# Idle products as planned and only wide, and the combinations of w_out on VectorE

## The chip, the cores and the metric

The kernel runs on one core of a Trainium2 chip. The metric is the device time of one execution in microseconds, taken as the median of several runs. A separate execution was recorded by the hardware profiler; its page and its trace are what is read here. TensorE appears in them as PE (its weight loads as PEld), VectorE as DVE, ScalarE as ACT, GpSimd as POOL, and SyncE, which here only issues DMAs, as SP. "Issue" is time in which an engine waited for nothing that the profile shows.

## The reference

A recurrent attention block feeds a dense block. For each of 4 batches and 8 heads, 768 steps go through a 48 x 48 state; the 3072 rows of the result (384 wide) then go through two weight matrices with a pointwise function between them. The weights come as 64-bit floats.

```python
for t in range(S):
    kt, vt, rt = (k[:, :, t], v[:, :, t], r[:, :, t])
    cur = np.einsum('bhd,bhe->bhde', u[None] * kt, vt)
    y[:, :, t] = np.einsum('bhd,bhde->bhe', rt, state + cur)
    state = w[None, :, :, None] * state + np.einsum('bhd,bhe->bhde', kt, vt)
...
h = x @ w_in                  # 3072 x 384 by 384 x 2048
g = h - np.tanh(h)
return (g @ w_out).astype(np.float32)   # 2048 x 384
```

## The kernel before

**Units.** The recurrence is cut into 64 steps of two batches: a unit, 24 in all. The function `unit` gives each its steps. TensorE turns r and k (L738); VectorE scales r by powers of the decay (L742), ScalarE copies k (L751) or VectorE scales it (L746). TensorE makes the products with the state and the levels, k against r within the 64 steps (both L693). VectorE copies the levels under a mask into `at` (L892), ScalarE writes the diagonal of `at` (L763). TensorE then makes the outputs and the state's increment (L693), ScalarE copies the output into `xt` and `rest` (L829), GpSimd issues six DMAs for every two units that move `rest` into place (L850), and VectorE adds to the state and decays it (L856, L901). Two states alternate, and all units share the product banks `yk_ps` and, for the first sixteen, `x_ps`. So the units run one behind the other.

**Dense tiles.** Two units make one column block j of 256 tokens, 12 in all. A tile is one j with two groups of 128 rows of the hidden layer. TensorE makes `h` in two halves (L166, three products each), ScalarE five functions of it (L175 to L183), VectorE four operations that end in `g` (L190 to L196; L190 reads `h` in PSUM, L192 and L194 read two SBUF tiles), and TensorE the product with `w_out` into `o` (L204). `h` has two banks, so the tile after next needs this tile's `h` read. The first six j are done in four passes over quarters of the hidden layer, with sums kept in `part` (L217). The last six j use seven products instead of eight (L254, banks `p`): GpSimd adds pieces of `g` into `sg` (L239 to L243), and combinations of `w_out`, called `mixed`, are made once for all, in 16 operations (`mixing`, L263; `mix` holds the formulas). `mixed` takes the place of the buffers of the weights' conversion, so it is made after the last conversion.

**Weights.** Sixteen pieces are loaded as 64-bit numbers by SP and GpSimd (L121) and made 32-bit floats by five operations of VectorE and two of ScalarE each (L135 to L141).

**The order.** Every step is put on a list with its engine, its cost and what it waits for (`add`). The class `Plan` then finds an order by hand-written simulation when the program is built: `forward` lays the steps out by due times, `order` tries 1000 random changes of these times and keeps those that end no later. Each engine's instructions stand in that order; nothing is reordered while the kernel runs. SP's loads are steps of the plan too, and each load waits for the one eight places ahead of it on its engine to land.

**Idle products.** In the opening TensorE has gaps, and the plan puts products into them whose result nobody reads (`fills`), into an `h` bank until the first `h`, then into an `x_ps` bank until the first `o`. There are wide ones of 512 columns (L630, `w_up` against the identity, planned at 0.9 us), which need `w_up`, and narrow ones of 128 (L631, identity against itself, planned at 0.25). `filled` counts how many fit between the end of the last step on TensorE and the start of the next. `forward` also plans TensorE's instruction fetch: it counts steps, and where a block of them ends, the end of the step can be put later:

```python
late = max(0.0, comes - crossed)
end += late
...
free[e] = end
```

When the plan is written out at the end of `order`, the gap is counted a second time, from

```python
free = t.start + t.cost
```

which is without `late`.

Of the kernel before, what the change touches and what calls it, by code (L numbers as in the profile page):

```python
# [143 lines left out]
class Dense:  # L144
# [112 lines left out]
    def mix(self, f, x):  # L257

        n, w, pairs = self.d.DM // 2, self.w_out_sb.rearrange("p (f z) n -> p f z n", z=2)[:, f], self.seven.mixed[:, f]
        b11, b12, b21, b22 = w[:, :, 0, :n], w[:, :, 0, n:], w[:, :, 1, :n], w[:, :, 1, n:]  # L260
        out, a, b, op = [(0, b11, b12, ALU.subtract), (1, b22, pairs[:, :, 0], ALU.add), (2, b22, b12, ALU.subtract),
                         (3, pairs[:, :, 1], b21, ALU.subtract)][x]
        self.nc.gpsimd.tensor_tensor(pairs[:, :, out], a, b, op)  # L263

    def collect(self, t, x):

# [29 lines left out]
class Plan:  # L296
# [14 lines left out]
    def add(self, engine, cost, run, after=(), due=1e9, data=0, gated=False, steps=0):  # L311
        t = SimpleNamespace(engine=engine, cost=cost, run=run, after=[x for x in after if x], due=due, data=data,
                            gated=gated, steps=steps, then=[], n=len(self.tasks))
        for x in t.after:
            x.then.append(t)
        self.tasks.append(t)
        return t
# [12 lines left out]
    def forward(self, due):  # L330

        ready = [max(self.FIRST, due[t.n] - self.EARLY) if t.gated else 0.0 for t in self.tasks]
        count = [len(t.after) for t in self.tasks]
        waiting = self.queues(ready, count)
        free, lanes, channel = dict(self.BEGIN), {}, 0.0
        step, bound, comes, fills = 0, self.CHUNK_0, 0.0, iter(self.fills)
        filling = next(fills, None)
        starts, done, last, first, changed = [None] * len(ready), [], 0.0, {}, set(waiting)
        while len(done) < len(ready):
            for e in changed:  # L340
                ts = waiting[e]
                first.pop(e, None)
                if not ts:
                    continue
                start = max(free.get(e, 0.0), min(ready[x.n] for x in ts))
                t = min((x for x in ts if ready[x.n] <= start + 1e-9), key=lambda x: (due[x.n], x.n))
                if t.data:
                    start = max(start, lanes.setdefault(e, [0.0] * self.LANES)[0])
                else:

                    soon = [x for x in ts if ready[x.n] < start + t.cost and due[x.n] < due[t.n] - self.SPARE]
                    if soon:
                        t = min(soon, key=lambda x: (ready[x.n], x.n))
                        start = max(start, ready[t.n])
                first[e] = start, t
            e = min(first, key=lambda x: (first[x][0], x))
            start, t = first[e]
            waiting[e].remove(t)
            changed = {e}
            end = start + t.cost  # L360
            if e == "PE":
                if filling:
                    step += 4 * len(self.filled(filling, free[e], start, starts))
                    if t is filling[1]:
                        filling = next(fills, None)
                step += t.steps
                if step >= bound:
                    each = t.cost / max(t.steps, 1)
                    crossed = end - (step - bound) * each
                    late = max(0.0, comes - crossed)  # L370
                    end += late
                    comes = max(crossed + late + self.ASKED * each + .3, channel) + self.COMES
                    bound += self.CHUNK
            free[e] = end
            if t.data:
                channel = max(channel, start + 1.2) + t.data
                end = max(end + self.LANDS, channel + self.LANDED) + self.slow(start)
                lanes[e] = lanes[e][1:] + [end]
            starts[t.n] = start
            last = max(last, end)  # L380
            done.append(t)
            for x in t.then:
                ready[x.n] = max(ready[x.n], end + self.hop(t, x))
                count[x.n] -= 1
                if not count[x.n]:
                    waiting[x.engine].append(x)
                    changed.add(x.engine)
        return last, starts, done
# [47 lines left out]
    def order(self, tries=1000):  # L436


        due = [t.due for t in self.tasks]
        for t in reversed(self.tasks):  # L440
            for x in t.then:
                due[t.n] = min(due[t.n], due[x.n] - t.cost - self.HOP - (self.LANDS if t.data else 0))
        plan = self.forward(due)
        for _ in range(4):
            due = self.backward(plan)
            plan = self.forward(due)
        chance = Random(5)
        for _ in range(tries):
            by, at, wide = chance.choice((0.3, 1, 2, 5)), chance.uniform(0, plan[0]), chance.choice((15, 40, 100, 700))
            moved = [x + chance.gauss(0, by) * (abs(start - at) < wide / 2) for x, start in zip(due, plan[1])]  # L450
            other = self.forward(moved)
            if chance.random() < .5:
                latest = self.backward(other)
                again = self.forward(latest)
                if again[0] < other[0]:
                    other, moved = again, latest
            if other[0] <= plan[0]:
                plan, due = other, moved
        self.due = due
        _, starts, done = plan  # L460
        free, order, fills = self.BEGIN["PE"], [], iter(self.fills)
        filling = next(fills, None)
        for t in done:
            t.start = starts[t.n]
            if t.engine == "PE" and filling:
                order += [SimpleNamespace(engine="PE", cost=0.0, start=free, run=run)
                          for run in self.filled(filling, free, t.start, starts)]
                if t is filling[1]:
                    filling = next(fills, None)
                free = t.start + t.cost  # L470
            order.append(t)
        return order

# [18 lines left out]
def near(ctx, tc, r, k, v, w, u, out, shared, moe_w_in, moe_w_out):  # L492
# [3 lines left out]
    V, A, T, G, Q = nc.vector, nc.scalar, nc.tensor, nc.gpsimd, nc.sync  # L496
    d = shared["dims"]
    H, D, NP, NK, B, HEAD = d.H, d.D, d.NP, d.NK, d.B, d.HEAD
    ident = shared["ident"]
# [13 lines left out]
    plan = Plan()  # L513
    add = plan.add
# [87 lines left out]
    w_up = fixed("w_up", [128, NP, 2, SHORT])  # L602
# [7 lines left out]
    idle, tab = (ps_d.tile([128, 2, d.NT], F32, name="h", tag="h") for _ in range(2))  # L610
    idle, tab = idle.rearrange("d z t -> d (z t)"), tab.rearrange("s z t -> s (z t)")
# [14 lines left out]


    def fills(to):
        wide = w_up.rearrange("d p z t -> d (p z t)")
        return [(.9, lambda: T.matmul(to, ident, wide, start=True, stop=True)),  # L630
                (.25, lambda: T.matmul(to[:, :128], ident, ident, start=True, stop=True))]  # L631


    now = [add(e, 1.25 if e == "ACT" else .87, lambda e=e, at=at, x=x: e_of[e].dma_start(out=rows[at : at + NP, :, :D], in_=x.rearrange("(p i) d -> p i d", i=2)), due=-1, data=.05)
           for e, at, x in (("SP", 0, w), ("ACT", NP, u))]
# [3 lines left out]
    now = add("DVE", .45, lambda: V.tensor_scalar(  # L639
        by[:, :, 1:], wcol[:, :, None].to_broadcast([128, NP, SHORT]), W_LOW, W_HIGH, ALU.max, ALU.min), [cols])  # L640
# [3 lines left out]
    ups = add("ACT", .6, lambda: A.copy(w_up, power[:, :, None, :SHORT].to_broadcast([128, NP, 2, SHORT])), [now])  # L644
# [28 lines left out]
    loads, converted = [], []  # L673
# [238 lines left out]
    def mixing():  # L912

        for f in range(0, d.NF // 2, 2):
            now = None
            for x in range(4):
                def run(f=f, x=x):
                    later()
                    dense.mix(slice(f, f + 2), x)

                now = add("POOL", 1.0, run, converted + [now])
            mixed.append(now)

    def finished_seven(t, x, due, pace):
# [11 lines left out]
    def hidden(j, fs, f, due, pace, seven=False):  # L936
# [8 lines left out]
        x.h = add("PE", 1.29, lambda: dense.h(t, 1), [now], due + 1.3, steps=12)  # L945
        last_h[j] = x.h
        if m == 0:
            plan.fills += [([], tabled, fills(idle)[1:]), ([ups], now, fills(idle))]
        x.s = add("ACT", .48, lambda: dense.act(t, "s"), [x.h, b2.c1, b2.q, b2.small, b1.s])
        x.th = add("ACT", .48, lambda: dense.act(t, "th"), [x.h, b2.g, b1.th] + ([units[m].rk, units[m].kw] if m < L else []))  # L950
        x.tg = add("ACT", .48, lambda: dense.act(t, "tg"), [x.h, b2.cp, b1.tg])
# [23 lines left out]
        for i in range(L):  # L975
            ends = SimpleNamespace()

            def run(i=i, ends=ends):
                dense.empty(t, i)
                ends.o = t.o  # L980
# [346 lines left out]
```

## Time and profile before

| | |
|---|---|
| median of 3 runs | 617.49 us (616.53 to 619.28) |
| profiled execution | 616.69 us |
| its span, first to last instruction | 615.0 us |
| mean granted TensorE clock | 0.991 |
| idle products, L631 / L630 | 72 passes of 128 / 24 passes of 512 |
| `mixed` on GpSimd, L263 | 16 operations in three groups: 10.9, 5.7 and 5.4 us busy |
| VectorE operation of the same shape, L867 | 0.58 us mean |

How to read it: a 32-bit product runs in two passes on TensorE, and the trace counts passes, so 72 passes are 36 products. A line of a timeline gives the start, the time until the last of its instructions ended, engine, line, operation, output and inputs, and in brackets the idle time before it with what ended it. A line of a table by stretches gives the stretch and its length, then busy time and number of instructions of PE, PEld, DVE, ACT and POOL, the granted clock, the DMA share and GB/s. A line of the waits gives the total, how often, and the longest.

### The profile page before, as it was taken

To read this page: it belongs to the slowest core of one execution; us is meant where nothing else is said; L and a number is where in the kernel's file an instruction comes from. 1 tells how busy PE (TensorE), PEld (TensorE's weight loads), DVE (VectorE), ACT (ScalarE), POOL (GpSimd) and SP (SyncE) were. 2 spreads that over 40 slices of the span, in tenths; PEclk is the share of its full clock that TensorE was granted. 3 is DMA by queue.
4 is the path that set the end of the run, shared out by engine and by line. 5 is a ranking of instruction groups with operands and counts; after the bars stand their busy time and mean duration, and the time that the engine had idled before them with its cause. 6 is when DMAs were issued, how large, how long until landed. Compare 5 with 4: busy or idle time off the path is not lost.

```text
span 615.0 us, 13927 instructions
## 1 busy us (share of the span) xinstructions
PE 596.4 (97%) x5499; PEld 483.4 (79%) x5499; DVE 453.5 (74%) x735; ACT 401.9 (65%) x896; POOL 177.1 (29%) x313
## 2 busy tenths in 40 slices
PE   8799999999999999997999999999999999999995
PEld 7477777667777777775777799889889899889993
DVE  5599888997789689996668765766786765645753
ACT  2498878878676567662557765675775666747652
POOL 5001311300000000193123452543362244436440
PEclk9899999999999999997999999999999999999999
DMA  7964686407024100002123410130120010100101
GB/s 128 219 126 88 129 161 166 90 0 174 8 46 102 52 0 2 0 14 52 38 52 82 82 23 0 37 57 19 26 58 17 15 27 7 23 6 8 26 2 30
DMA packets 86323, 33.73 MB, mean 55 GB/s; under 512 B 78537, under 2 KB 80681, under 8 KB 86249
## 3 DMA queue, kind: packets, MB, share of 16 engines
q1 hardware_dynamic: 81084, 25.57, 20.7%
q0 software_dynamic: 4992, 6.99, 5.2%
q8 instruction: 45, 0.74, 0.5%
q14 instruction: 30, 0.24, 0.1%
q10 hardware_dynamic: 172, 0.20, 0.1%
HBM read 26.94 MB, written 4.72 MB: 51 GB/s over the span
## 4 chain that ended last, share of the span: by engine, by line
PE 79%; DVE 9%; ACT 5%; issue 3%; DMA 2%; SPq 1%; DVEq 0%; ACTq 0%
PE h L166 36%; PE p L254 17%; PE o L204 16%; PE yk_ps L693 5%; DVE rT L742 1%; DVE tg L194 1%; PE yk_ps L738 1%; DVE tg L192 1%; PE h L630 1%; SPq L726 1%; ACT at L763 1%; PE p L204 1%; PE x_ps L738 1%; DVE g L196 1%; DMA kt<-in_k_dram 1%
## 5 line engine op out<-in xcount | busy, mean ns | idle before, releaser
L166 PE MATMUL h<-xt,w_in_sb 128*128 128x256 f32 x1152 | 282.4, 382 | 0.2 <-DVE w_in_sb L141 0.2
L166 PEld LDWEIGHTS h<-xt,w_in_sb 128*128 128x128 f32 x1152 | 214.6, 191 | 42.7 <-issue 1.0
L204 PE MATMUL o<-w_out_sb,g 128*128 128x384 f32 x384 | 142.0, 493 | 0.5 <-DVE g L196 0.3
L192 DVE SCALAR_TENSOR_TENSOR tg<-s,tg 128x512 f32<-128x512 f32 x96 | 68.7, 716 | 58.8 <-ACT tg L179 44.4
L190 DVE TENSOR_TENSOR g<-h,th 128x512 f32<-128x512 f32 x96 | 65.9, 686 | 43.0 <-ACT s L175 32.2
L204 PEld LDWEIGHTS o<-w_out_sb,g 128*128 128x128 f32 x384 | 72.0, 191 | 32.5 <-DVE g L196 1.4
L179 ACT ACTIVATE tg<-h 128x512 f32<-128x512 f32 x96 | 57.2, 595 | 53.7 <-PE h L166 53.7
L175 ACT ACTIVATE s<-h 128x512 f32<-128x512 f32 x96 | 57.3, 596 | 49.7 <-PE h L166 49.7
L177 ACT ACTIVATE th<-h 128x512 f32<-128x512 f32 x96 | 57.1, 595 | 32.0 <-PE h L166 31.9
L196 DVE COPY_PREDICATED g<-small,tg 128x512 f32<-128x512 int32 x96 | 73.2, 763 | 5.0
L194 DVE SCALAR_TENSOR_TENSOR tg<-q,tg 128x512 f32<-128x512 f32 x96 | 69.6, 725 | 6.1 <-ACT q L181 2.6
L239 POOL TENSOR_TENSOR sg<-g 128x256 f32<-128x256 f32 x46 | 35.2, 766 | 132.3 <-DVE g L196 123.0
L181 ACT ACTIVATE q<-s,m1b 128x512 f32<-128x512 f32 x96 | 69.5, 724 | 0.5
L183 ACT ACTIVATE small<-s,smallb 128x512 f32<-128x512 f32 x96 | 69.4, 723 | 0.5
L254 PE MATMUL p<-mixed,sg 128*128 128x192 f32 x276 | 67.4, 326 | 0.0
L850 POOL DMA_DIRECT2D xt<-rest x66 | 32.4, 497 | 91.8 <-ACT rest L829 91.6
L763 ACT ACTIVATE at<-same,du 128x64 f32<-128x64 f32 x184 | 47.6, 341 | 4.9 <-DVE du L759 4.7
L254 PEld LDWEIGHTS p<-mixed,sg 128*128 128x128 f32 x276 | 48.7, 190 | 0.0
L254 PE MATMUL p<-w_out_sb,g 128*128 128x192 f32 x184 | 46.2, 333 | 0.0
L254 PEld LDWEIGHTS p<-w_out_sb,g 128*128 128x128 f32 x184 | 33.2, 190 | 4.3
L263 POOL TENSOR_TENSOR mixed<-w_out_sb 128x384 f32<-128x384 f32 x8 | 10.9, 1378 | 77.2 <-DVE w_out_sb L141 77.2
L829 ACT COPY xt<-yk_ps 64x192 f32<-64x192 f32 (+2 forms) x50 | 16.2, 323 | 23.7 <-PE yk_ps L693 23.3
(136 smaller groups left out, 694.4 us busy)
## 6 DMA issues: line engine op xcount, KB each, us to landing
st<-in_moe_w_out_dram SPq DMA_DIRECT2D x8, 768.0 KB, 7.3
rt<-in_r_dram SPq DMA_DIRECT2D x48, 96.0 KB, 2.9
vt<-in_v_dram SPq DMA_DIRECT2D x48, 96.0 KB, 3.0
st<-in_moe_w_in_dram SPq DMA_DIRECT2D x16, 288.0 KB, 6.4
kt<-in_k_dram SPq DMA_DIRECT2D x44, 96.0 KB, 2.9
out_dram<-part POOLq DMA_DIRECT2D x24, 96.0 KB, 2.2
out_dram<-o POOLq DMA_DIRECT2D x20, 96.0 KB, 2.1
st<-in_moe_w_in_dram POOLq DMA_DIRECT2D x16, 96.0 KB, 3.9
```

What stands on the lines that cost most here:

```text
L166: self.nc.tensor.matmul(t.h2[:, z], self.w_in_sb[:, t.f // 2, kk, z * 128 : (z + 1) * 128], self.xts[t.j][:, kk].rearrange("p b t -> p (b ...
L175: A.activation(out, t.h, AF.Square)
L177: A.activation(out, t.h, AF.Tanh)
L179: A.activation(out, t.h, AF.Tanh, scale=G1)
L181: A.activation(out, t.s, AF.Square, bias=self.m1b)
L183: A.activation(out, t.s, AF.Relu, bias=self.smallb, scale=-1.0)
L190: V.tensor_tensor(t.g, t.h, t.th, ALU.subtract)
L192: V.scalar_tensor_tensor(t.tg, t.s, C4, t.tg, ALU.mult, ALU.mult)
L194: V.scalar_tensor_tensor(t.tg, t.q, K1, t.tg, ALU.add, ALU.mult)
L196: V.copy_predicated(t.g, t.small.bitcast(I32), t.tg)
L204: self.nc.tensor.matmul(self.outs[i], t.g2[:, z, i * C : (i + 1) * C], self.w_out_sb[:, t.f + z, :], start=t.first and z == 0, stop=t.last ...
L254: self.nc.tensor.matmul(ps[bank][:, half * n : (half + 1) * n], a, b, start=t.first and half == 0, stop=t.last, skip_group_check=True)
```

## The change

Three things are done. `order` runs `forward` once more on the times it chose, and `forward` keeps for each step of TensorE which idle products it counted in front of it (`fitted`); these are the ones written out. The idle products become 512 columns (planned at 0.9) or 256 columns (planned at 0.46), both the identity against itself repeated, so they need no `w_up` and come from one list from the start to the first `h`. And the 16 combinations of `w_out` are steps of VectorE, planned at 0.47 each, instead of GpSimd, planned at 1.0. Since costs and steps differ, the search ends in another order of all engines' instructions.

```diff
@@ mix
-        self.nc.gpsimd.tensor_tensor(pairs[:, :, out], a, b, op)
+        self.nc.vector.tensor_tensor(pairs[:, :, out], a, b, op)
@@ forward
+        self.fitted = []
...
                 if filling:
-                    step += 4 * len(self.filled(filling, free[e], start, starts))
+                    runs = self.filled(filling, free[e], start, starts)
+                    self.fitted.append((free[e], t.n, runs))
+                    step += 4 * len(runs)
@@ order
-        free, order, fills = self.BEGIN["PE"], [], iter(self.fills)
-        filling = next(fills, None)
+        self.forward(due)
+        fitted, order = {n: (free, runs) for free, n, runs in self.fitted}, []
         for t in done:
             t.start = starts[t.n]
-            if t.engine == "PE" and filling:
-                order += [SimpleNamespace(engine="PE", cost=0.0, start=free, run=run)
-                          for run in self.filled(filling, free, t.start, starts)]
-                if t is filling[1]:
-                    filling = next(fills, None)
-                free = t.start + t.cost
+            free, runs = fitted.get(t.n, (0.0, [])) if t.engine == "PE" else (0.0, [])
+            order += [SimpleNamespace(engine="PE", cost=0.0, start=free, run=run) for run in runs]
             order.append(t)
@@ fills
-        wide = w_up.rearrange("d p z t -> d (p z t)")
-        return [(.9, lambda: T.matmul(to, ident, wide, start=True, stop=True)),
-                (.25, lambda: T.matmul(to[:, :128], ident, ident, start=True, stop=True))]
+        def run(n):
+            T.matmul(to[:, : n * 128].rearrange("p (n m) -> p n m", n=n), ident, ident[:, None, :].to_broadcast([128, n, 128]),
+                     start=True, stop=True)
+
+        return [(.9, lambda: run(4)), (.46, lambda: run(2))]
@@ mixing
-                now = add("POOL", 1.0, run, converted + [now])
+                now = add("DVE", .47, run, converted + [now])
@@ hidden
-            plan.fills += [([], tabled, fills(idle)[1:]), ([ups], now, fills(idle))]
+            plan.fills.append(([], now, fills(idle)))
```

## The prediction

> **What bounds the kernel now.** I read the page's busy shares first, then the waits of the matmul queue, then busy time by stretch, and at last the timelines where a stretch is not full.
>
> ```profile
> PE 596.4 (97%) x5499; PEld 483.4 (79%) x5499; DVE 453.5 (74%) x735; ACT 401.9 (65%) x896; POOL 177.1 (29%) x313
> ```
>
> TensorE is busy nearly always, and its real work is not changed. So only three things can move: idle products, TensorE's idle time, and work at a lowered clock. Its waits, longest in total first:
>
> ```profile
> PE yk_ps L693 <- DVE at L892: 4.0, 3, 3.3
> PE x_ps L693 <- issue: 3.7, 1, 3.7
> ```
>
> Two single waits stand out. The first, by stretches of 4 us (columns: PE, PEld, DVE, ACT, POOL busy, then granted clock):
>
> ```profile
> 276.00:280.00 4.00, 4.00 (x75) 2.75 (x74) 4.00 (x5) 0.96 (x2) 4.00 (x4) 1.00 0.00 0
> 280.00:284.00 4.00, 0.65 (x6) 0.07 (x6) 3.96 (x7) 0.00 (x0) 1.36 (x3) 0.92 0.00 0
> 284.00:288.00 4.00, 4.00 (x68) 3.00 (x69) 1.33 (x3) 2.00 (x8) 1.22 (x3) 0.50 0.59 127
> 288.00:292.00 4.00, 4.00 (x13) 2.79 (x12) 0.59 (x2) 1.67 (x7) 0.00 (x0) 0.73 0.41 74
> ```
>
> TensorE idles while VectorE is full, and then runs at half clock. The timelines (VectorE, then TensorE) say why:
>
> ```profile
> 267.74 0.69 DVE L190 TENSOR_TENSOR g<-h,th 128x512 f32<-128x512 f32 x1 [0.33 <-ACT tg L179]
> 268.35 1.46 DVE L192 SCALAR_TENSOR_TENSOR tg<-s,tg 128x512 f32<-128x512 f32 x1
> 269.92 1.30 DVE L194 SCALAR_TENSOR_TENSOR tg<-q,tg 128x512 f32<-128x512 f32 x1
> ...
> 291.97 0.69 DVE L192 SCALAR_TENSOR_TENSOR tg<-s,tg 128x512 f32<-128x512 f32 x1 [2.84 <-ACT tg L179]
> ```
> ```profile
> 283.93 1.14 PE L693 MATMUL yk_ps<-at,vt 64*64 64x64 f32 x32 [3.35 <-DVE at L892]
> 284.85 1.05 PE L693 MATMUL yk_ps<-vt,kw 64*64 64x48 f32 x32
> 285.83 2.93 PE L204 MATMUL o<-w_out_sb,g 128*128 128x384 f32 x4
> 288.55 2.27 PE L166 MATMUL h<-xt,w_in_sb 128*128 128x256 f32 x6
> ```
>
> While GpSimd makes `mixed` (258.96 to 280.4), VectorE's products of two SBUF tiles take up to 1.46 us instead of 0.69; L190, with one operand in PSUM, stays at 0.69. VectorE falls behind and the copy L892 comes late.
>
> The second wait, in TensorE's timeline:
>
> ```profile
> 16.17 0.34 PE L693 MATMUL x_ps<-rT,kT 48*64 48x64 f32 x6
> 20.20 0.77 PE L693 MATMUL x_ps<-rT,kT 48*64 48x64 f32 x26 [3.70 <-issue]
> 20.91 6.90 PE L630 MATMUL h<-w_up,ident 128*128 128x512 f32 x12
> 27.65 0.38 PE L631 MATMUL h<-ident 128*128 128x128 f32 x2
> 27.96 0.58 PE L693 MATMUL yk_ps<-at,vt 64*64 64x64 f32 x24
> ```
>
> TensorE stops within unit 1's levels with nothing that the profile shows to wait for, then runs six wide idle products, although unit 1's copy L892 was done at 22.2 (21.48 + 0.72). They hold the unit for 5.8 us.
>
> **What the Trainium skill says.** "GPSIMD Engine Reference", § 8 Key points: GpSimd shares SBUF interfaces with VectorE, contending with instructions in a two-port mode or with two SBUF inputs. The trace agrees (1.46 against 0.69, L190 untouched). "TensorE: Matmul & The Clock Gate", What's actually happening: an idle window of about 3.4 us halves the clock, about 3.4 us of work restores it. Here 3.35 us idle gave 0.50, and 1.00 came back by 292. "Runtime: NRT & Kernel Launch", Instruction fetch mechanics: instructions come in blocks of 256, mostly hidden. Here one fetch, as I read the wait, cost 3.70 us.
>
> **The combinations move to VectorE.** Removed: 16 GpSimd operations, 10.9 + 5.7 + 5.4 = 22.0 us busy (three groups of L263), on no path of their own. What they cost is the 3.35 us wait plus the slow work after it: 64 passes of L693 in 1.96 instead of 1.15, an `o` pair in 2.86 instead of 1.29, an `h` half in 2.06 instead of 1.29 (chain of waits), together 0.81 + 1.57 + 0.77 = 3.15. In sum 6.5 us. Added: 16 VectorE operations of 128x384, two SBUF inputs. The nearest row is L867, 0.55 to 0.58 us each and 0.47 from start to start when queued: 16 x 0.47 to 16 x 0.58 = 7.5 to 9.3 us. By the order of the built program they stand one to four at a time between five dense tiles. A tile costs TensorE 4 x 1.29 = 5.17 us there, and VectorE 4 x 0.62 + 2 x 0.47 + 4 x 0.47 = 5.3: even. Between the end of a tile's `h` and its `o`, the new order has 12.9 us of TensorE work (before, in its mixing stretch: 5.2 to 7.8), so a lag of a tenth of a microsecond a tile is covered. Without that cover it would cost up to 9.3; I take 0. GpSimd's queue loses operations that stood ahead of output DMAs only. Gain: 6.5 (bounds 3.3, if the clock still falls for another reason, and 6.5).
>
> **The idle products.** Before: 36 of 128 columns and 12 of 512, 10,752 columns. After: 13 of 512 and 8 of 256, 8,704. The first 1,024 columns, at half clock, are equal and take 3.7 us in both (1.52 to 5.24). The other 2,048 go at 1.79 us for eight of 128 (7.75 to 9.54), 3.6 us; and the six behind the fetch ran slow, 6.74 instead of 6 x 0.9. Some 4.9 us of filling go, and idle time may take its place; so I walk the units by hand, with the durations above.
> Up to the stop TensorE had made 219 passes, 46 of them idle products; now those are 16. The stop therefore comes 30 passes later, behind unit 1's levels, in the idle products that follow. If the block lands at about 20.2 as before, unit 1's outputs start near 20.5 instead of 27.96. Then unit 2's state products near 25.5 (32.26 before); its outputs near 28.1 (37.71), held by VectorE's second L135, which waits for weights that SP now issues near 18.5, behind the operands of units 1 and 2; I let them land at 25.3. Next the first `h`, both halves, near 30.7, behind L141; unit 3 at 33.3 (43.37); unit 4 at 40.5 (50.95); the last idle product ends near 42.4 (53.09 before).
> Not all of that is gain. At unit 4 the new order has two `h` halves less done (2.6 us), and from there VectorE sets the pace: in 40 to 53 it was busy 12.73 of 13, in 53 to 70 16.53 of 17. In my walk the first `o` comes at 51.5, with about 4.8 us more of TensorE work done than before at that time, and before then lost 1.1 more: 5.9. Counted on VectorE, the lead is one unit, 6 x 0.47 + 2 x 0.62 = 4.1. Between the two I take 4.5 (bounds 0 and 8: no lead survives, or unit 1's 7.5 with no loss).
> The new order also has tight places. From the last first-stage tile's `h` to its `o` there are 5.1 us of work, and from the first `h` of the seven products to `p` 7.3 (9.9 before), with GpSimd's 0.77 + 0.53 + 0.56 in between. I charge 1.0 (bounds 0 and 6.5, a stall like the one removed). The tail, from the last `p` products on, stands in the same order: 0. SP's loads are reordered in the opening only, which the walk holds.
>
> **Sum.** 6.5 + 4.5 - 1.0 = 10.0 us. The profiled execution took 616.69 with a span of 615.0, so 1.69 lies around it: 605.0 + 1.69 = 606.7. The median of the three runs is 0.8 above that execution: 607.5.
>
> **Rivals.** (1) Only the combinations help: VectorE, full from 40 to 70, eats the opening. For it: its share there. Against: it idled 3.48 us before 31.25 and 2.20 before 20.61 for TensorE and ScalarE. 617.5 - 6.5 + 0.5 = 611.5. (2) The stall comes back where units 12 to 15 meet the seven products: 6.5 + 4.5 - 6.5 leaves 613, and with no opening gain 617.5. For it: 5.1 and 7.3 us. Against: before, tiles with 5.2 us passed with 0.91 us idle in 100 to 150. (3) Slower: fewer idle products let the clock fall in the opening. Place: the gaps up to the last idle product. Each fall costs 3.15, as measured above. Against 10 us of gain it decides from four falls on; five give 617.5 - 10 + 15.8 = 623. For it: 3.7 us idle already gave 0.78 in 20.2 to 28. Against: the gaps that I find are under 3 us, but for the fetch. That the change doesn't do what it says: the order shows 16 L263 on VectorE and the counts above, so no.
>
> **How the numbers follow.** The forecast, 604 to 611: 0.58. Rival 1, 610 to 613: 0.22. Rival 2: 0.12, of which half stays within 0.5% (3.1 us, about what a measurement of this kernel can tell from no change). Rival 3 and other slower cases: 0.08. So faster 0.58 + 0.22 + 0.05 = 0.85, less 0.02 for rival 1's upper end: 0.83; same 0.09; slower 0.08. The range takes in the forecast, rival 1 and the better half of rival 2: 602 (opening at its bound of 8 and the tight places at nothing: 617.5 - 14.5 = 603, and a microsecond for the median) to 614.5.
>
> **What would show it.** Right: no wait over 1 us between 230 and 300, L192 at 0.7 throughout, clock 1.00 there; unit 1's outputs near 20.5; the last idle product before 45; GpSimd near 155 us busy. Wrong: a stretch with a clock below 0.8 after 30; TensorE waiting on VectorE's L263; the wait of L135 for weights past 30; a wait over 2 us at the first `p`.

## The result and the profile after

| | before | after |
|---|---|---|
| median of the runs on one chip | 618.27 us (616.53 to 619.28, 4 runs) | 609.56 us (608.24 to 610.10, 4 runs) |
| profiled execution, its span | 616.69 us, 615.0 us | 610.10 us, 608.3 us |
| TensorE busy, and span less busy | 596.4, 18.6 us | 589.8, 18.5 us |

The ratio is 0.9859 (95% interval 0.9828 to 0.989): about 8.7 us less, where 10.0 were forecast. The profiled execution is the longest of the four and the one before (616.69) close to the shortest, so the pair of traces shows less gain (6.7 us of span) than the medians.

The last row of the table is the first thing to read. The whole gain is busy time; the idle time is as long as before, although both waits shown before are gone. Other waits have come. First the busy shares on the page, then TensorE's waits (total, how often, longest):

```profile
PE 589.8 (97%) x5445; PEld 474.8 (78%) x5445; DVE 456.3 (75%) x751; ACT 400.8 (66%) x896; POOL 152.6 (25%) x297
```
```profile
PE h L629 <- issue: 2.2, 1, 2.2
PE yk_ps L694 <- issue: 2.0, 1, 2.0
PE p L204 <- DVE e L284: 1.7, 1, 1.7
PE yk_ps L694 <- DVE at L893: 1.6, 3, 1.0
PE yk_ps L694 <- DVE state L857: 1.5, 3, 0.8
```

In the opening one wait for nothing but issue has become two, which together (4.2) are longer than the 3.70 of before. A third, of 1.13 us, stands at 101.3. The wait for the copy of the levels (L892 before, now L893) is down from 4.0 in three to 1.6 in three. First the stretch from 250 to 300 us before the change, then the same after it, and from 276 to 292, the four windows of the prediction in one:

```profile
250.00:300.00 50.00, 46.65 (x293) 34.00 (x293) 40.35 (x53) 27.54 (x56) 25.57 (x24) 0.93 0.12 24
```
```profile
250.00:300.00 50.00, 50.00 (x198) 36.92 (x197) 43.61 (x73) 31.35 (x55) 5.23 (x10) 1.00 0.09 19
276.00:292.00 16.00, 16.00 (x63) 11.67 (x62) 14.66 (x27) 8.73 (x15) 3.85 (x8) 1.00 0.17 38
```

TensorE is full and its clock is 1.00 where it had stood at 0.50. VectorE has more to do and does it sooner:

```profile
271.39 0.73 DVE L196 COPY_PREDICATED g<-small,tg 128x512 f32<-128x512 int32 x1
272.02 0.55 DVE L263 TENSOR_TENSOR mixed<-w_out_sb 128x384 f32<-128x384 f32 x1
272.48 1.02 DVE L263 TENSOR_TENSOR mixed<-w_out_sb,mixed 128x384 f32<-128x384 f32 x2
273.41 0.55 DVE L263 TENSOR_TENSOR mixed<-w_out_sb 128x384 f32<-128x384 f32 x1
273.88 0.69 DVE L192 SCALAR_TENSOR_TENSOR tg<-s,tg 128x512 f32<-128x512 f32 x1
```

A combination takes about 0.5 us from start to start where GpSimd took 1.4 on average (22.0 us for 16), and L192 beside it takes 0.69, not 1.46. The opening, on TensorE:

```profile
16.33 0.69 PE L694 MATMUL x_ps<-rT,kT 48*64 48x64 f32 x32
16.96 1.98 PE L629 MATMUL h<-ident 128*128 128x512 f32 x4
21.14 0.59 PE L629 MATMUL h<-ident 128*128 128x256 f32 x2 [2.20 <-issue]
21.66 0.58 PE L694 MATMUL yk_ps<-at,vt 64*64 64x64 f32 x24
...
29.56 0.27 PE L694 MATMUL yk_ps<-rT,state 48*64 48x64 f32 x1 [1.97 <-issue]
29.56 0.73 PE L694 MATMUL x_ps<-rT,kT 48*64 48x64 f32 x32
30.22 2.29 PE L629 MATMUL h<-ident 128*128 128x512 f32 x4
32.84 1.13 PE L694 MATMUL yk_ps<-at,vt 64*64 64x64 f32 x32 [0.33 <-DVE at L893]
...
35.57 2.83 PE L166 MATMUL h<-xt,w_in_sb 128*128 128x256 f32 x12
...
56.20 1.56 PE L204 MATMUL o<-w_out_sb,g 128*128 128x384 f32 x4
```

Unit 1's levels run in one piece, the stop falls into idle products behind them, and unit 1's outputs come at 21.66 instead of 27.96. Then a second stop of 1.97 us falls into unit 2's state products. The first `o` comes at 56.20, later than before (53.09), but with more of the other work done by then.

Where the busy time went (596.4 to 589.8, 6.6 us less): the idle products, summed over their groups, went from 26.2 to 21.4 (4.8 less), and the slow work behind the old stall is gone (3.15 less). Against that, unit 2's outputs now run at a lowered clock, 1.13 + 0.89 us instead of 0.69 + 0.63, which is 0.7 more. That makes 7.25; 0.65 of the difference I can't place.

### The profile page after: what moved, and what is told of

The parts are those of the page before. It is cut to its first block, busy times and chain, and to the rows that moved or that the text cites. A ratio compares the mean times of both kernels' runs of the same rounds, so it can differ in the third digit from the quotient of the medians.

```text
span 608.3 us, 13833 instructions
## 1 busy us (share of the span) xinstructions
PE 589.8 (97%) x5445; PEld 474.8 (78%) x5445; DVE 456.3 (75%) x751; ACT 400.8 (66%) x896; POOL 152.6 (25%) x297
## 3 DMA queue, kind: packets, MB, share of 16 engines
q1 hardware_dynamic: 81084, 25.57, 21.4%
## 4 chain that ended last, share of the span: by engine, by line
PE 82%; DVE 6%; DMA 3%; ACT 3%; SPq 3%; issue 2%; DVEq 0%; POOL 0%; POOLq 0%
PE h L166 38%; PE o L204 19%; PE p L254 17%; PE yk_ps L694 5%; SPq L727 2%; DMA st<-in_moe_w_in_dram 2%; PE yk_ps L739 1%; ACT at L764 1%; DVE rT L743 1%; PE p L204 1%; DMA kt<-in_k_dram 1%; PE x_ps L739 1%; ACT kT L752 1%; SPq L121 1%; PE x_ps L694 1%
## 5 line engine op out<-in xcount | busy, mean ns | idle before, releaser
L192 DVE SCALAR_TENSOR_TENSOR tg<-s,tg 128x512 f32<-128x512 f32 x96 | 68.9, 718 | 47.4 <-ACT tg L179 29.1
L190 DVE TENSOR_TENSOR g<-h,th 128x512 f32<-128x512 f32 x96 | 65.9, 687 | 38.8 <-ACT s L175 16.5
L196 DVE COPY_PREDICATED g<-small,tg 128x512 f32<-128x512 int32 x96 | 70.9, 738 | 5.4 <-ACT small L183 0.3
L194 DVE SCALAR_TENSOR_TENSOR tg<-q,tg 128x512 f32<-128x512 f32 x96 | 66.4, 692 | 6.2 <-ACT q L181 2.8
L290 POOL DMA_DIRECT2D out_dram<-part x24 | 12.6, 528 | 144.2 <-DVE part L217 144.2
```

The lines of the kernel that those rows point to most:

```text
L190: V.tensor_tensor(t.g, t.h, t.th, ALU.subtract)
L192: V.scalar_tensor_tensor(t.tg, t.s, C4, t.tg, ALU.mult, ALU.mult)
L194: V.scalar_tensor_tensor(t.tg, t.q, K1, t.tg, ALU.add, ALU.mult)
L196: V.copy_predicated(t.g, t.small.bitcast(I32), t.tg)
```

## The experiments

The times of runs that went to the chip together share the runs of the kernel before (median 619.0, 618.7, 619.6 and 619.4 in the four sets), so what is compared is the ratio to it. In each kernel all instructions but the ones named stand in the order of the kernel it is made from.

### The two parts apart

**b_mix_vector**: the kernel before, the combinations on VectorE, nothing else.

```diff
-        self.nc.gpsimd.tensor_tensor(pairs[:, :, out], a, b, op)
+        self.nc.vector.tensor_tensor(pairs[:, :, out], a, b, op)
```

> The order of before, with only the 16 combinations issued on VectorE at the places that the plan gave them on GpSimd. Theory A (the gain is GpSimd's contention with VectorE, whatever the order): the 3.35 us wait and the half clock go, 6.5 us faster than before, about 611.5; L192 at 0.7 throughout. Theory B (the gain is the new order's longer distance from h to o): 16 more VectorE operations at distances of 5.2 us bring a wait of their own, 0 to 3 us faster, 615 or more.

**b_fills_as_planned**: the kernel before, its own idle products (128 and 512 wide), but placed as the planner counted them.

```diff
+                    runs = self.filled(filling, free[e], start, starts)
+                    self.fitted.append((free[e], t.n, runs))
...
-            if t.engine == "PE" and filling:
-                order += [SimpleNamespace(engine="PE", cost=0.0, start=free, run=run)
-                          for run in self.filled(filling, free, t.start, starts)]
...
+            free, runs = fitted.get(t.n, (0.0, [])) if t.engine == "PE" else (0.0, [])
+            order += [SimpleNamespace(engine="PE", cost=0.0, start=free, run=run) for run in runs]
```

> The order of before, with only the count of idle products as the plan had it, in the old widths (6 wide ones behind the fetch become 1, and one wide and two narrow ones go later). If the opening's lead lasts (the 4.5 us of the forecast): 613 to 614. If the opening waits for loads and VectorE instead: unit 1's outputs start near 22.5 instead of 27.96, but within 1.5 us of before, about 617.

**b_both**: both edits on the order of before.

> The order of before with both edits. If the parts add up: the sum of the two gains, 610 to 611 where the opening gives 1 us, 607 where it gives 4.5. If this equals the changed kernel, its new order as such is worth nothing.

**a_mix_gpsimd**: the changed kernel, the combinations back on GpSimd.

```diff
-        self.nc.vector.tensor_tensor(pairs[:, :, out], a, b, op)
+        self.nc.gpsimd.tensor_tensor(pairs[:, :, out], a, b, op)
```

> The changed kernel's order, with only the 16 combinations issued on GpSimd. Theory A: the wait and the slow clock come back, 5 to 7 us slower than the changed kernel, about 615 to 616. Theory B: 12.9 us from h to o cover VectorE's slow operations, within 1.5 us of the changed kernel, 609 to 611, with L192 near 1.4 us all the same.

| run | median us | ratio to before |
|---|---|---|
| b_mix_vector | 615.41 (612.98 to 617.54, 12 runs) | 0.9936 [0.9917, 0.9956] |
| b_fills_as_planned | 614.05 (613.11 to 615.99, 6 runs) | 0.9931 [0.9905, 0.9956] |
| b_both | 609.85 (608.59 to 612.28, 6 runs) | 0.9864 [0.9837, 0.9891] |
| a_mix_gpsimd | 613.29 (612.31 to 615.74, 6 runs) | 0.992 [0.9893, 0.9947] |

The parts add: 0.64% and 0.69% make 1.33%, and both together gave 1.36%, which is the changed kernel's 1.41% within the intervals. So the new order of the work, which the diff brings along, is worth nothing that can be measured here. The combinations are worth 4.0 us (0.64% of 619; from the changed kernel backwards 0.61%, 3.8 us), the idle products 4.3. The expectations of b_fills_as_planned (613 to 614) and b_both (the parts add) held. The other two had two theories each. The 3.6 to 4.0 us of b_mix_vector are less than theory A's 6.5 and more than theory B's 0 to 3, and a_mix_gpsimd's 613.29 lies between its two, for the reasons that follow.

Why 4.0 and not the 6.5 of the forecast? First the line of 250 to 300 us, from b_mix_vector, then its wait for the copy:

```profile
250.00:300.00 50.00, 48.84 (x314) 35.77 (x314) 42.90 (x75) 29.15 (x59) 4.20 (x8) 1.00 0.14 29
```
```profile
PE yk_ps L693 <- DVE at L892: 1.8, 3, 1.2
```

The clock holds, so the slow work is gone, but 1.2 us of the 3.35 stay: VectorE is still late at the same copy, now with its own combinations ahead of it. By this trace and the first one of before the move is worth 3.15 + 2.15 = 5.3 us; the runs say 2.7 to 5.1. The other profile of the kernel before, before_again, shows why the forecast read too much:

```profile
285.61 1.13 PE L693 MATMUL yk_ps<-at,vt 64*64 64x64 f32 x32 [3.33 <-DVE at L892]
286.52 1.05 PE L693 MATMUL yk_ps<-vt,kw 64*64 64x48 f32 x32
287.50 2.16 PE L204 MATMUL o<-w_out_sb,g 128*128 128x384 f32 x4
289.50 1.46 PE L166 MATMUL h<-xt,w_in_sb 128*128 128x256 f32 x6
```

The stall is the same, but the clock is back sooner: `o` takes 2.16 us instead of 2.93, and `h` is at full speed. In the chain of waits the slow work comes to 1.6 us (1.96 + 2.09 + 1.29 against 1.15 + 1.29 + 1.29) instead of 3.15. In b_fills_as_planned, with a stall of 3.32, it comes to 1.8. With these the move is worth about 3.8 and 3.9 us. So 4.0 is about what stall and slow work come to when the first profile isn't the only one asked. A smaller part lies outside the span: the runs of b_mix_vector have 2.3 to 2.6 us there, those of before 1.7; the cause of that is open.

In the changed kernel's order the stretch is full, but there GpSimd does less harm to begin with. From a_mix_gpsimd, the waits, the same stretch, and VectorE's slowest operation in it:

```profile
PE o L204 <- DVE part L217: 2.5, 3, 1.3
```
```profile
250.00:300.00 50.00, 47.52 (x186) 34.38 (x185) 44.47 (x54) 28.75 (x50) 22.85 (x24) 1.00 0.07 16
```
```profile
283.05 5.86 DVE L196 COPY_PREDICATED g<-small,tg 128x512 f32<-128x512 int32 x1
```

Three waits of at most 1.3 us, and the clock stays at 1.00 (a wait of 3.35 us had halved it). VectorE was held up even more at one place, 5.86 us in a copy that takes 0.73 without GpSimd beside it, and TensorE's longest wait behind it was 1.05 us. That the 12.9 us between `h` and `o` of this order take up the lag fits this; no run changes that distance alone. So the full price of 6.5 is met in neither order.

The idle products, TensorE's timeline of b_fills_as_planned behind the stop:

```profile
22.39 1.01 PE L692 MATMUL x_ps<-rT,kT 48*64 48x64 f32 x26 [6.12 <-issue]
23.33 2.07 PE L629 MATMUL h<-w_up,ident 128*128 128x512 f32 x2
```

Two passes (one product) stand where twelve stood, 2.07 us instead of 6.90. That is the gain, and it comes although this execution's stop was 2.4 us longer than before's. Planned and written placement now agree, which is the part of the diff that acts; that the products are wider is not needed for it.

### The stops for issue

> The changed kernel once more, unaltered, for a second execution's profile and beside the run above on one chip. Theory 'the instruction fetch's wait differs from execution to execution at the same place': the waits of TensorE for nothing but issue (2.2 us ahead of L629 at 21.1 and 2.0 us ahead of L694 at 29.6 in the first profile) differ by 0.5 us or more in at least one place, and the span by about as much; the median is 608.5 to 610.5. Theory 'it is fixed by the program': the two waits are within 0.3 us of the first profile's.

> The kernel before once more, unaltered, for a second execution's profile. Theory 'the wait differs from execution to execution': the wait for issue in the opening (3.70 us in the first profile) is another by 0.5 us or more, the wait of 3.35 us ahead of L693 near 284 and the half clock behind it are the same within 0.3 us of length. Theory 'fixed by the program': 3.4 to 4.0 us.

| kernel (profile) | waits for issue in the opening, us | span |
|---|---|---|
| before | 3.7 | 615.0 |
| before_again | 4.8 | 616.8 |
| b_mix_vector, same instructions up to there on TensorE | 5.7 | 612.6 |
| after | 2.2 and 2.0 | 608.3 |
| after_again | 1.5 and 1.7 | 607.9 |

after_again took 610.04 us (608.57 to 611.48, 6 runs; ratio 0.9854 [0.9826, 0.9882]), before_again 618.55. In both the theory held that the length differs from execution to execution. The place is fixed by the program, the length is not: 3.7 to 5.7 at one place of one TensorE program, and b_fills_as_planned and b_both had 6.12 and 4.25 there. Counted in the traces, 219 passes stand ahead of the first stop in before and after alike (46 and 20 of them idle ones), and 346 ahead of the second one. In before_again the stall near 284 was 3.3 us again. A single profile can't price an edit of the opening to better than 2 us, then; the ratios above are what prices it.

### The idle products as such

**a_no_idle**: the changed kernel, no idle product written out. Their result is read by nothing.

```diff
-            order += [SimpleNamespace(engine="PE", cost=0.0, start=free, run=run) for run in runs]
```

> The changed kernel without any idle products (they write only to banks that nothing reads, so the outputs are unaffected): 20.9 us of TensorE work gone from the opening, the order of everything else as it was. Theory 'they hold the clock' (rival 3 of the prediction taken to its end): the granted clock stands near 0.5 over most of 10-50 us, unit 1's and unit 2's products and the first h take twice their time, the first o comes 4 to 10 us later than 56.2 and the median is 614 to 620. Theory 'they are only in the way' (the opening is set by loads, by instruction fetches and by VectorE): the clock falls there too, but the first o comes no later than 57 and the median is 606 to 611.

612.44 us (611.46 to 613.18, 6 runs), ratio 0.9902 [0.9876, 0.9929]: 2.7 us (0.43%) slower than the changed kernel, between the two theories. TensorE in its timeline:

```profile
36.61 3.97 PE L166 MATMUL h<-xt,w_in_sb 128*128 128x256 f32 x12
...
47.73 0.69 PE L693 MATMUL yk_ps<-rT,state 48*64 48x64 f32 x32 [2.96 <-DVE state L856]
...
50.50 2.90 PE L166 MATMUL h<-xt,w_in_sb 128*128 128x256 f32 x6 [1.60 <-DVE w_in_sb L141]
53.32 1.13 PE L693 MATMUL yk_ps<-at,vt 64*64 64x64 f32 x32
...
60.34 1.56 PE L204 MATMUL o<-w_out_sb,g 128*128 128x384 f32 x4
```

Slow work stands at two places. Up to the first `h` the products take up to twice their time (the `h` passes from 36.61 on 3.97 us instead of 2.83), and unit 3 starts 2.2 us later than in the changed kernel, at 40.51. The clock on record is 1.00 there, so it doesn't show this part; in a_no_idle_loads, where the products of that stretch are as slow, it is 0.50 from 20 to 36 us. Then the 2.96 us without work at 47.7 are followed by a clock of 0.62 in the stretch from 48 to 57: six passes of `h` take 2.90 instead of 1.53, the outputs behind them 1.13 instead of 0.69, and the first `o` comes at 60.34 instead of 56.20. These 4.1 us stay to the end. The two profiles differ by 3.1 us of span only because the stop of 1.13 us for issue at 101.3 is absent here. So the products do hold the clock, but by the runs 20 us of them buy less than 3 us. A good part of the slow work runs where TensorE waited for data anyway, 3.48 us for the copy L892 ahead of unit 2's outputs, for instance.

### The late weights

In the changed kernel VectorE waits to 30.25 us for the second piece of w_in. Its queue is in order, so the first piece's L139 and unit 2's copy stand behind that wait. In its profile:

```profile
30.25 0.56 DVE L135 TENSOR_SCALAR power<-st 128x768 uint32<-128x768 uint32 x1 [4.34 <-DMA st<-in_moe_w_in_dram]
```

**a_loads** moves one DMA on SP, the first load of w_out, behind the two loads of the second piece of w_in (`pieces[n]` are the load steps of piece n):

```diff
-    for t in plan.order():
+    order = plan.order()
+    order.remove(pieces[2][0])
+    order.insert(order.index(pieces[1][2]) + 1, pieces[2][0])
+    for t in order:
```

> The changed kernel with one DMA moved: SP issues the first load of w_out (st, one transfer of all 128 partitions) behind the two loads of the second piece of w_in instead of ahead of vt and of them. Theory 'the second piece's landing decides the opening' (the term that the prediction's walk had at 25.3 and the trace at 30.25): VectorE's wait at L135 ends 2 to 3.5 us earlier, at 27 to 28; unit 2's outputs come at 31 to 32.5 and the median falls by 0.5 to 2 us, to about 608. Theory 'the second instruction fetch and the idle products behind it decide': L135 starts earlier all the same, unit 2's outputs stay within 0.5 us of 32.8 and the median within 0.5 us of the changed kernel's (609.6).

> The run with the load of w_out moved, once more and unaltered, on another chip, to see whether its 608.2 (ratio 0.9848) against 609.6 to 610.0 (0.9859 and 0.9854) of the changed kernel is more than spread. Theory 'the landing is worth 1 us or more': 607.5 to 609 and a ratio of 0.983 to 0.9855 again. Theory 'what comes early waits elsewhere': 609.3 to 610.5, ratio 0.9855 to 0.988. In both the wait for the second piece's weights at VectorE's L135 ends at 27 to 28 us, not at 30.

608.17 us (607.40 to 610.66, 6 runs; ratio 0.9848 [0.9818, 0.9879]) and, on another chip, 608.87 (607.38 to 610.78, 6 runs; 0.9835 [0.9802, 0.9867]). VectorE's wait in the first (lines are one or two further down in these kernels), then TensorE in the second:

```profile
27.42 0.56 DVE L135 TENSOR_SCALAR power<-st 128x768 uint32<-128x768 uint32 x1 [1.73 <-DMA st<-in_moe_w_in_dram]
```
```profile
30.39 0.27 PE L695 MATMUL yk_ps<-rT,state 48*64 48x64 f32 x1 [2.44 <-issue]
30.40 0.73 PE L695 MATMUL x_ps<-rT,kT 48*64 48x64 f32 x32
31.06 2.76 PE L629 MATMUL h<-ident 128*128 128x512 f32 x4
33.74 1.10 PE L695 MATMUL yk_ps<-at,vt 64*64 64x64 f32 x32
```

The weights land 2.8 us earlier. In the first profile the second stop was absent and unit 2's outputs came at 31.36; in the second it was there, and with the four passes of idle products behind it the outputs came at 33.74, later than in the changed kernel. The twelve times fall into two clusters, eight of 607.4 to 609.1 and four of 610.5 to 610.8; the two profiled executions, 608.0 and 610.55, lie one in each. Their spans differ by 2.6 us: 1.75 up to the first `o`, and 0.9 behind it, where the second has a stop of 1.0 us for issue at 101.8 and the first none. That these stops part the clusters is likely, with two profiles not shown. Over both sets the mean is 608.9 (12 runs) against 609.7 of the changed kernel (10 runs): a gain of 0.8 us is the estimate, and the intervals overlap.

**a_no_idle_loads**: both edits.

> Both edits together: no idle products, and the load of w_out behind those of w_in. If the four idle products between unit 2's levels and its outputs (30.2 to 32.5 us) hid the earlier landing, this is 1 to 2 us faster than the better of the two single edits (about 605 to 608). If the clock needs the idle products, it is as slow as the run without them (614 to 620), within 1 us. If the fetches decide, it equals the run without idle products within 0.5 us.

611.86 us (610.97 to 612.10, 5 runs), ratio 0.9889 [0.986, 0.9918]: as slow as without idle products alone (0.9902), within the intervals. The "four idle products" of this expectation are four passes, so two products; without them the earlier landing brought no gain that can be told from spread, although the first `o` came at 58.51 instead of 60.34 in the profiles.

**a_loads_vec**: a_loads, and on VectorE unit 2's copy and unit 3's kw ahead of the first piece's L139, unit 3's rk behind its L141.

```diff
+    for t, at in ((units[2].cp, parts[0][4]), (units[3].kw, parts[0][4]), (parts[0][6], units[3].rk)):
+        order.remove(t)
+        order.insert(order.index(at), t)
```

> The run with the load of w_out moved, and VectorE's order mended around 28-34 us: unit 2's copy_predicated (cp) and unit 3's kw come ahead of the first piece's L139 (the multiply that waits for ScalarE's st), L139, L140 and L141 then follow each other, and unit 3's rk comes behind them. Theory 'VectorE's in-order queue is what is late next in the opening': cp at 29.0 instead of 30.6, unit 2's outputs at 29.6 instead of 31.4, the first h at 32.8 instead of 34.2, and the median 1 to 1.5 us below the run with the load alone (608.2), about 607. Theory 'a later link (the state products of units 3 and 4, or a fetch) ends last whatever comes early': the first h comes earlier, the first o does not, and the median stays within 0.5 us of 608.2.

611.01 us (609.87 to 614.06, 6 runs), ratio 0.9881 [0.9849, 0.9913], beside 610.04 of after_again on the same chip: no gain. Its profile has the second stop (1.9 us), so the copy waited for TensorE's levels until 30.39, the first `h` came at 34.43 (34.19 in a_loads) and the first `o` at 55.13, as in a_loads. So the edit didn't bring the first `h` earlier, and neither theory was put to the test. The median lies 2.8 us above that of a_loads. In the profiles the spans differ by 2.4, all of it behind the first `o`: 0.7 at a stop for issue at 99.9, which a_loads's doesn't have, and 1.7 in the last 16 passes of `p`, which took 7.32 us instead of 5.63, with a clock of 0.55 from 598 to 601. Whether that holds for the other runs is open.

### Another order

**a_seed6**: the changed kernel, the planner's search with another seed.

```diff
-        chance = Random(5)
+        chance = Random(6)
```

> The changed kernel with another seed for the planner's random search and nothing else: another order of the same work. Theory 'the order as such is worth nothing measurable, the two edits are': within 2.5 us of the changed kernel (607 to 612). Theory 'the change's gain is the luck of one search': 4 us or more away from it, 614 or later.

611.29 us (610.69 to 613.95, 6 runs), ratio 0.99 [0.987, 0.993]. Within the 2.5 us: most of the gain stays with another order. The 0.4% between the two ratios is what one draw of the search made here, over half of what one of the two edits gave.

The fastest kernel measured is a_loads, by an amount that is not shown to be more than spread.

## Why the prediction was right, point by point

**The sum.** 10.0 us forecast, 8.7 measured (9.0 in the second set). The forecast time, 607.5, stood on a median of three runs, 617.49; longer sets of the same kernel gave 618.3 to 619.6. So 607.5 against 609.56 is 1.3 us of too much gain, and the rest is the base.

**Combinations, 6.5: right mechanism, mis-sized term.** Measured: 4.0. GpSimd's work beside VectorE was the cause: "GPSIMD Engine Reference", § 8 Key points, says that the two contend when VectorE's operation has two inputs in SBUF, and without the combinations on GpSimd L192 is back at 0.69 us and the clock at 1.00. L190, with one input in PSUM, took 0.69 with and without. The size was wrong in two parts. I booked the whole stall as gain, though VectorE was to get 7.5 us of work in the same stretch, and in before's order 1.2 us of it stay. And I booked 3.15 us of slow work from one execution, where two others with the same stall show 1.6 and 1.8. In the new order GpSimd would have cost 3.8.

**The cost of sixteen operations on VectorE, 0: right in the new order**, where 250 to 300 is full; not in the old one, where the 1.2 us remain. The cover I named, 12.9 us between `h` and `o`, is the likely reason, but the orders differ in more than that: the sixteen also stand closer together in the old one (262 to 280 us, against 268 to 289), and no run takes the two apart.

**Idle products, 4.5: right size (4.3 on the old order), the walk half right.** The stop did come behind unit 1's levels, and the 4.8 us of filling that went are the 4.9 of the forecast. The times of the walk were too early: unit 1's outputs 21.66 (20.5), unit 2's 32.84 (28.1), the first `h` 35.57 (30.7), the first `o` 56.20 (51.5), the end of the last idle product 48.27 (42.4). Two steps of it failed. The second stop was not in it, and the weights landed at 30.25, not 25.3: SP issued them at 20 to 21 us, not 18.5, and the transfer took 9.46 us in the chain of waits. From the first `o` on, 542.4 us busy are left against 550.4 before, of which 3.15 were slow work: 4.9 us. So the opening won 53.09 - 56.20 + 4.9 = 1.8 us in this pair of profiles, where the walk had 5.9 by the same count. before_again and after_again give 54.77 - 55.84 + 4.9 = 3.8 (542.4 us left against 550.6, with 1.6 of slow work behind the stall and 1.7 in the last products). The 4.5 was a mean of two counts, 4.1 and 5.9; that it came so near to the 4.3 of the runs is partly luck. Rival 1, that the opening gives nothing, is excluded by b_fills_as_planned.

**Tight places, 1.0: not where I had them.** Between 101.3 and 407.3 us TensorE has no wait over 0.15, so neither of the places I named cost anything. Two new waits of a microsecond came elsewhere, at L893 after 400 us and for issue at 101.3. The order as such measured as nothing (b_both 0.9864, changed 0.9859), and a charge of 1.0 lies within these intervals. Rival 2, a return of the long stall, did not come.

**Rival 3, the clock in the opening.** Two of my signs against the forecast appeared: L135 waited past 30, and the clock stood at 0.71 in 32 to 36 us. One of those for it did not: the last idle product ended behind 45. None of them decided anything. I had priced each fall of the clock at 3.15 us; with no idle product at all the loss was 2.7 in sum, since slow work in an opening with waits is, as I read it, partly hidden. A sign needs a price beside it to be one.

**The fetch.** I took "Runtime: NRT & Kernel Launch", Instruction fetch mechanics, for the reading of the 3.70 us stop. The traces agree that it falls at a fixed count: the first stop has 219 passes ahead of it in eleven profiles, whatever number of them are idle ones, and the second has 346 in seven. The 127 passes between, each with its weight load, are 254 instructions, close to the block of 256 that the page names. That TensorE waits for a fetch is still a reading; no trace shows what ends the stop. That it is mostly hidden isn't so in this opening, where the stops that show lasted 0.3 to 6.1 us.

## What to carry to other kernels

When an edit takes a slow neighbour away, book the stall only as far as the engine behind it would then be in time: run its own queue forward with the added work and see what wait remains. Read the price of a stall from more than one execution: here the wait was the same each time and the slow work behind it was not. Measure parts of a change on the old order of work before crediting a new order; here the two edits on the old order gave the whole gain. Work put in to keep a clock up is worth only what runs on the path, so price it by taking all of it out once.

## What was not expected of the hardware

- The stop for issue lasted 3.7, 4.8, 5.7, 6.1 and 4.2 us at the same place of five executions with the same 219 passes ahead of it on TensorE. A second one, 127 passes on, was there in after, after_again, a_mix_gpsimd, a_loads_again2 and a_loads_vec (1.7 to 2.4 us) and absent in a_loads.
- VectorE's operations with two SBUF inputs doubled beside GpSimd (1.46 against 0.69 us, one copy even 5.86 against 0.73), in one order enough for a stall of 3.35 us and half the clock, in another order only for waits of up to 1.3 us, without any fall of the clock.
- How long the clock stayed down behind the same wait differed between executions. Behind a stall of 3.3 us the slow work cost 3.15, 1.6 and 1.8 us. Behind a last wait of 1.66 us, which before and before_again both have, the last 16 passes took 5.63 us in the one and 7.32 in the other.
